# Two groups of filler matmuls divided otherwise near the end of a fused attention and soft-MoE kernel

## The chip, the cores and the metric

The kernel runs on one core of one Trainium2 chip. The core has a matrix engine (TensorE, in the profile PE for its matmuls and PEld for its weight loads), VectorE (DVE), ScalarE (ACT), GpSimd (POOL) and SyncE (SP, which here only issues DMAs), and 16 DMA engines. The metric is the device time of one execution in microseconds (us). Before the change the median of 4 runs is 302.89 us, with 301.69 us the lowest and 304.32 us the highest.

## What is computed

The reference is attention with a soft cap on the scores, whose output is the input of a mixture of experts with soft slots:

```
scores = cap * tanh(q @ k^T / sqrt(64) / cap)          # 8 batches x 12 heads, 448 x 448, cap = 30
attn   = softmax(scores) @ v                           # head size 64
x      = attn, heads side by side                      # 3584 tokens x 768
logits = x @ phi                                       # 3584 x 32 slots, 8 experts with 4 slots each
d = softmax over the tokens;  c = softmax over the slots
slot_input = d^T @ x                                   # 32 x 768
slot_out[e] = relu(slot_input[e] @ w1[e]) @ w2[e]      # hidden size 1024
out    = c @ slot_out                                  # 3584 x 768, float32
```

## The kernel before

The attention covers 48 pairs of heads. Each pair has 7 tiles of 64 keys from each head of 448 keys, which makes 336 tiles, taken in an order that interleaves the two pairs of a quad. Six tiles are a chunk, so there are 56 chunks (NCH = 56, numbered 0 to 55). For a chunk TensorE makes scores in two halves of three tiles (`qk_chunk`, L316), ScalarE applies tanh (`tanh_chunk`, L325) and, for most tiles, exp (`exp_part`, L329). In some chunks one or two tiles get their exp as a polynomial on VectorE instead (`poly_exp`, L359 to L364). Two chunks later TensorE multiplies the result with v (`pv_mms`, L382), VectorE divides by the row sums (`norm`, L389 and L392), and GpSimd casts the next v (`vcast`, L286).

Everything that is not in this main loop hangs on named slots. `at(j, slot, f, ...)` puts a call into chunk j's slot, and `run(j, slot)` issues it when the loop comes by. The order of work on every engine is thus written out by hand: an engine takes its instructions in this order, and nothing rearranges them later. The slot "d" of a chunk comes after the second `qk_chunk` of that chunk, so at the very end of it; the next thing on TensorE that needs its own place is `pv_first` in the chunk after.

Among the calls are filler matmuls, whose results nobody reads. `fill` adds them into unused columns of the bank of the product with v. `spare(n, parts)` takes a tile of 128 x (128 * parts) from the pool `psV`, with the tag "pv", and calls `busy(n, tile)`. That pool has one buffer, so a `spare` tile has to wait until VectorE has read the product with v before it, and the next product with v has to wait until the filler is written. In `busy` a tile wider than 128 columns is served with n // 3 matmuls of 384 columns (L626) and n % 3 of 128 columns (L629). A tile of 128 columns is served with n matmuls of 128 columns (L629). Each matmul has a weight load of its own ahead of it.

After the last chunk come the last two pairs' products with v (tiles `pvm` and `pvl`), the last logits and slot sums (`slpl`), the experts' first layer (`layer1`, tile `hp`, L820, in four groups of 24 matmuls: two halves for experts 0 to 3, two for experts 4 to 7), its relu (L831 on ScalarE, L834 on VectorE), the second layer (`layer2`, `so_ps`, L853) and the output (L885 to L945). The second layer's weights were partly put aside in DRAM and come back as `w2t` by DMAs that SP issues (L799). The output is 3584 x 768 float32, stored from L869 and L886.

Of the kernel before, what the change touches and what calls it, by code (L numbers as in the profile page):

```python
# [36 lines left out]
def kernel(  # L37
# [27 lines left out]
    NCH = NTILE // CH  # L65
# [473 lines left out]
    def at(j, slot, f, *a):  # L539
        if j < 0:  # L540
            j, slot = 0, "b"
        aux.setdefault((j, slot), []).append((f, a))
# [21 lines left out]
    for b in range(B):  # L564
        j, p = b * PER, 6 * b
# [36 lines left out]
        at(1 + n * (NCH - 5) // len(wjobs), "b", *job)  # L602
    for j, slot, n in ((0, "a", 10), (0, "c", 10), (1, "b", 10), (1, "c", 8)):
        at(j, slot, spare, n, 1)
    for j, slot, n, parts in ((NCH - 6, "d", 8, 3), (NCH - 4, "d", 8, 3), (NCH - 2, "d", 12, 1)):
        at(j, slot, spare, n, parts)
    at(0, "c", init_vbd, 0)
    at(1, "c", init_vbd, 1)
# [376 lines left out]
```

## Time and profile before

| | |
|---|---|
| median of 4 runs | 302.89 us (301.69 to 304.32) |
| the profiled execution | 302.53 us |
| its span, from first to last instruction | 300.7 us |
| TensorE matmuls busy | 266.2 us, 4828 matmuls, 4828 weight loads |
| ScalarE busy | 265.0 us |
| VectorE busy | 231.2 us |
| GpSimd busy | 137.6 us |
| DMA | 68.52 MB, mean 228 GB/s |
| 384-column fillers L626 on `junk` | 67 matmuls, 14.2 us busy |
| 128-column fillers L629 on `junk` | 77 matmuls, 8.1 us busy |

The span lies 1.8 us below the profiled execution's time; what is outside it is start and end of the program. Busy time is the union of an engine's instructions, so that matmuls which overlap in the array count once. The profile gives each matmul the time from its start until its result is complete, which is longer than the distance at which the next one can follow. A line of a timeline has start, duration, engine, source line, operation, output and inputs, and how many instructions it merges; in brackets stands the idle time before it and what ended it. In the chain of work that ended last, "issue" is time in which an engine waited for nothing that the profile shows.

### The profile page before, as it was taken

To read this page: it belongs to the slowest core of one execution; us is meant where nothing else is said; L and a number is where in the kernel's file an instruction comes from. 1 tells how busy PE (TensorE), PEld (TensorE's weight loads), DVE (VectorE), ACT (ScalarE), POOL (GpSimd) and SP (SyncE) were. 2 spreads that over 40 slices of the span, in tenths; PEclk is the share of its full clock that TensorE was granted. 3 is DMA by queue.
4 is the path that set the end of the run, shared out by engine and by line. 5 is a ranking of instruction groups with operands and counts; after the bars stand their busy time and mean duration, and the time that the engine had idled before them with its cause. 6 is when DMAs were issued, how large, how long until landed. Compare 5 with 4: busy or idle time off the path is not lost.

```text
span 300.7 us, 10911 instructions
## 1 busy us (share of the span) xinstructions
PE 266.2 (89%) x4828; PEld 180.0 (60%) x4828; DVE 231.2 (77%) x397; ACT 265.0 (88%) x211; POOL 137.6 (46%) x200
## 2 busy tenths in 40 slices
PE   8898889998999999989999999899999999898720
PEld 5665566755775667566756665667666777442400
DVE  3717869799988998899989988998888854237830
ACT  4999999999999999999999999999999996137720
POOL 4583563864486457634764567365633310300000
PEclk9999999999999999999999999999999999999985
DMA  7999999999999999999999999999999479939995
GB/s 253 243 187 205 193 196 208 186 216 219 208 202 195 198 228 219 195 204 229 180 190 209 226 193 194 215 223 211 191 210 199 128 235 348 413 128 381 407 421 233
DMA packets 58703, 68.52 MB, mean 228 GB/s; under 512 B 4256, under 2 KB 54688, under 8 KB 58656
## 3 DMA queue, kind: packets, MB, share of 16 engines
q0 software_dynamic: 42448, 35.31, 76.6%
q1 hardware_dynamic: 15920, 32.28, 30.7%
q8 instruction: 38, 0.62, 0.8%
q10 hardware_dynamic: 288, 0.23, 0.2%
q14 instruction: 9, 0.07, 0.1%
HBM read 92.11 MB, written 19.66 MB: 372 GB/s over the span
## 4 chain that ended last, share of the span: by engine, by line
ACT 42%; PE 30%; DVE 15%; issue 4%; POOL 3%; DMA 2%; DVEq 0%; SPq 0%; ACTq 0%; POOLq 0%
ACT ex L325 22%; ACT ex L329 17%; PE pv L382 9%; PE sc L316 4%; DVE ex L364 2%; DVE xq L392 2%; DVE work L363 2%; PE so_ps L853 2%; PE hp L820 2%; POOL vbd L286 2%; PE xps L430 2%; PE pv L412 1%; DVE work L362 1%; PE kps L276 1%; ACT ob L945 1%
## 5 line engine op out<-in xcount | busy, mean ns | idle before, releaser
L325 ACT ACTIVATE ex<-sc 128x1344 bf16<-128x1344 f32 (+1 forms) x113 | 144.0, 1353 | 1.8 <-PE sc L316 1.8
L329 ACT ACTIVATE ex<-ex 128x2688 bf16<-128x2688 bf16 (+5 forms) x58 | 120.9, 2093 | 0.1
L382 PE MATMUL pv<-vbd,ex 128*128 128x130 bf16 (+1 forms) x1610 | 95.4, 211 | 8.5 <-POOL vbd L286 5.9
L382 PEld LDWEIGHTS <-ex 128*128 128x128 bf16 (+1 forms) x1680 | 76.1, 101 | 34.1 <-issue 9.1
L316 PE MATMUL sc<-qT,kT 64*64 64x448 bf16 x672 | 71.3, 359 | 1.6 <-ACT ex L325 0.6
L286 POOL CAST vbd<-vraw 64x896 bf16<-64x896 f32 x46 | 45.0, 978 | 52.5 <-PE pv L382 38.4
L364 DVE SCALAR_TENSOR_TENSOR ex<-work 128x896 bf16<-128x896 f32 (+1 forms) x31 | 31.3, 1009 | 0.2
L363 DVE SCALAR_TENSOR_TENSOR work<-work 128x896 f32<-128x896 f32 (+1 forms) x31 | 30.2, 974 | 0.1
L362 DVE SCALAR_TENSOR_TENSOR work<-work 128x896 f32<-128x896 uint16 (+1 forms) x31 | 30.2, 973 | 0.0
L392 DVE TENSOR_TENSOR xq<-pv,rec 128x448 bf16<-128x448 f32 x46 | 28.7, 624 | 1.5
L316 PEld LDWEIGHTS <-kT 64*64 64x64 bf16 x672 | 23.6, 105 | 6.4 <-issue 2.9
L116 POOL DMA_DIRECT2D w1b<-in_moe_w_dram x32 | 24.8, 776 | 0.0
L474 POOL COPY e<-E 128x512 bf16<-128x512 bf16 x9 | 6.6, 731 | 39.0 <-PE eps L493 21.0
L294 POOL MEMSET vbd<- 64x1 bf16 x22 | 2.1, 96 | 47.3 <-PE pv L382 47.3
L278 DVE COPY kT<-kps 128x896 bf16<-128x896 bf16 x23 | 14.2, 618 | 10.0 <-PE kps L276 9.9
L361 DVE TENSOR_SCALAR work<-work 128x896 uint16<-128x896 uint16 (+1 forms) x31 | 20.8, 670 | 0.4
L412 PE MATMUL pv<-ones 128*128 128x57 bf16 x496 | 20.6, 188 | 0.0
L443 DVE COPY xT<-xps 128x896 bf16<-128x896 bf16 (+1 forms) x24 | 14.3, 598 | 8.0 <-PE xps L435 8.0
L359 DVE TENSOR_SCALAR work<-ex 128x896 int32<-128x896 bf16 (+1 forms) x31 | 20.2, 652 | 0.1
L186 POOL DMA_DIRECT2D qb<-in_q_dram x22 | 16.6, 754 | 3.1 <-DVE kT L237 3.1
L412 PEld LDWEIGHTS <-ones 128*128 128x128 bf16 x496 | 17.4, 96 | 0.3
L120 POOL DMA_DIRECT2D w2d<-in_moe_w_dram x22 | 16.8, 786 | 0.0
(130 smaller groups left out, 329.7 us busy)
## 6 DMA issues: line engine op xcount, KB each, us to landing
w1b<-in_moe_w_dram POOLq DMA_DIRECT2D x32, 384.0 KB, 8.7
vraw<-in_v_dram SPq DMA_DIRECT2D x44, 224.0 KB, 6.0
w2d<-in_moe_w_dram POOLq DMA_DIRECT2D x22, 384.0 KB, 8.7
w2t<-w2d SPq DMA_DIRECT2D x22, 384.0 KB, 7.3
out_dram<-ob SPq DMA_DIRECT2D x7, 768.0 KB, 8.4
qb<-in_q_dram POOLq DMA_DIRECT2D x22, 224.0 KB, 7.6
kb<-in_k_dram POOLq DMA_DIRECT2D x22, 224.0 KB, 6.0
out_dram<-obh SPq DMA_DIRECT2D x23, 192.0 KB, 2.0
```

The lines of the kernel that those rows point to most:

```text
L116: pool.dma_start(out=w1b[e][:, js, fs], in_=w1r[:, e, js, fs])
L286: pool.tensor_copy(vbds[Q % 2][r, :, :, c0:c0 + DH], raw[r])
L316: pe.matmul(sc[cs, u, 0:S], qkT["k", Q][r, c, cs], qkT["q", Q][r, :, cs], start=True, stop=True)
L325: act.activation(exs[j][:, half * CS + u0:half * CS + u1, :], sc[:, u0:u1, 0:S], ACT.Tanh, scale=qk_scale / cap)
L329: act.activation(exs[j][:, u0:u1, :], exs[j][:, u0:u1, :], ACT.Exp, scale=cap)
L361: lambda: dve.tensor_scalar(b.bitcast(U16), w, 7, None, ALU.logical_shift_left),
L362: lambda: dve.scalar_tensor_tensor(p, f, p2, f, ALU.add, ALU.mult),
L363: lambda: dve.scalar_tensor_tensor(p, p, p1, f, ALU.add, ALU.mult),
L364: lambda: dve.scalar_tensor_tensor(t, p, p0, b, ALU.add, ALU.mult))
L382: pe.matmul(out_, exs[j][r, u, q0:q0 + (HP if tail else P)], v_, start=(c == 0 and g == gs[0] < NF), stop=(c == NT - 1), skip_group_check= ...
L392: dve.tensor_tensor(xq[Q][:, h, s0:s1, :], pv[:, 0:s1 - s0, 0:DH], rec.to_broadcast([P, s1 - s0, DH]), op=ALU.mult)
L412: pe.matmul(home, ones, ones[:, 0:512 - NT * W], start=False, stop=True, skip_group_check=True)
```

## The change

One line of the table that places three of the `spare` calls is changed:

```
-    for j, slot, n, parts in ((NCH - 6, "d", 8, 3), (NCH - 4, "d", 8, 3), (NCH - 2, "d", 12, 1)):
+    for j, slot, n, parts in ((NCH - 6, "d", 11, 3), (NCH - 4, "d", 8, 3), (NCH - 2, "d", 12, 3)):
         at(j, slot, spare, n, parts)
```

In chunk 50 the filler is 11 units of 128 columns where it was 8: three matmuls of 384 columns and two of 128, where there were two and two. In chunk 54 the filler keeps 12 units, but on a tile of 384 columns: four matmuls of 384 columns, where there were twelve of 128. Chunk 52's filler is the same. On TensorE the program has one matmul and one weight load more in chunk 50, and eight of each less in chunk 54: 9658 become 9644. The other engines have the same instructions in the same order.

## The prediction

> **What bounds the kernel now.** I read the page's slices first, for where each engine is full, then the chain that ended last around the two places, then TensorE's timeline there, and last the DMA queues.
>
> The page's rows of busy time in 40 slices of 7.5 us:
>
> ```profile
> PE   8898889998999999989999999899999999898720
> ACT  4999999999999999999999999999999996137720
> PEclk9999999999999999999999999999999999999985
> ```
>
> Chunk 50's filler runs at 227 us and chunk 54's at 245 us, in slices 31 and 33. ScalarE is full in both, and TensorE nearly so. ScalarE's last exp ends at 252.08 us, while TensorE still multiplies that chunk with v until 253.9, so from there on TensorE is the late one. The chain, in order of time, agrees:
>
> ```profile
> 241.00 0.79 PE pv L382 x12
> ...
> 243.43 0.77 PE pv L382 x11
> 244.55 0.64 DVE xq L392
> 245.23 0.86 PE junk L629 x12
> 246.13 0.84 PE pv L382 x12
> ...
> 257.45 2.72 PE hp L820 x48
> 260.16 1.04 issue
> 261.20 1.48 PE hp L820 x24
> ```
>
> Here the filler of chunk 54 is itself a link, between VectorE's division and the next product with v. Ten us later there is a hole of 1.04 us, "issue", between the second and third group of the experts' first layer. After it the chain goes on to the output, whose stores start at 268.7 us and keep the DMA engines full to 297 us, so what comes late at 261 us ends late.
>
> TensorE's timeline at the two fillers, and one from 217 us with four wide ones:
>
> ```profile
> 217.00 0.82 PE L626 MATMUL junk<-ones 128*128 128x384 bf16 x4
> ...
> 226.97 0.50 PE L626 MATMUL junk<-ones 128*128 128x384 bf16 x2
> 227.31 0.28 PE L629 MATMUL junk<-ones 128*128 128x128 bf16 x2
> 227.64 0.84 PE L382 MATMUL pv<-vbd,ex 128*128 128x130 bf16 x12
> ...
> 245.23 0.84 PE L629 MATMUL junk<-ones 128*128 128x128 bf16 x12 [0.40 <-DVE xq L392]
> 246.13 0.84 PE L382 MATMUL pv<-vbd,ex 128*128 128x130 bf16 x12
> ```
>
> **Chunk 54.** Twelve narrow fillers take 0.84 us, the last 0.22 of it the last one's own time, so they start (0.84 - 0.22) / 11 = 56 ns apart. By the first row wide ones start about (0.82 - 0.33) / 3 = 163 ns apart, the first distance of a group being 10 ns longer. The product with v waits until the last filler is written: 246.13 is 56 ns after 245.23 + 0.84. Four wide ones end at 245.23 + 0.17 + 2 x 0.163 + 0.326 = 246.05, and v follows at 246.11. The change is worth **-0.02 us**. That eight weight loads go too is worth nothing: narrow fillers run at one per 56 ns with a load each, so the loads are hidden behind the columns.
>
> **Chunk 50.** One wide filler more: **+0.163 us**. It stands ahead of the next product with v at 227.64. The cover would be ScalarE, which is fed two halves ahead and does not wait for TensorE between 215 and 252 us; but TensorE's later waits in this stretch (0.19 us at 231.64 for GpSimd's v, 0.40 at 245.23 for VectorE) are for work that TensorE's own products released, and move along. So I take it in full. The bounds are 0, if those loops had room, and 0.163.
>
> Up to 255 us the sum is +0.14 us.
>
> **The hole at 260.16.** The third group's first matmul waits by the program for TensorE's own earlier writes only, and those are complete at 260.11. What else can hold it is the program itself:
>
> ```profile
> q8 instruction: 38, 0.62, 0.8%
> ```
>
> This queue brings code: 38 packets of 16 KB. TensorE's 9684 instructions, its semaphore ones included, make 255 a packet, so I take this as TensorE's code in blocks of 256. I set the packets' starts in the trace against the number of TensorE instructions started by then. All 38 lie at or behind the counts 256 k - 64, by 0.26 to 4.13 us (median 2.7), as if each block were asked for when the one before is entered. One of these counts, 9152, is exactly the first matmul after the hole. Its block was due when count 8896 was passed, at 254.70 us; its packet started at 258.77 (4.07 us later), took 0.93, and the matmul went at 261.20, 1.50 us after that. In the other 36 such spans TensorE reached the next count 1.36 us or more after the packet's end, so nothing stood still. Here it runs 256 instructions in 5.4 us, while the DMA engines carry 412 GB/s, and the late packet shows.
>
> Without the hole the third group would start at about 260.17, so the hole costs 1.04 us.
>
> The change moves the instructions behind chunk 54 forward by 14 counts. The boundary then falls 14 instructions later in the work, before the eighth matmul of the third group, and the request is due at what was count 8910, the logits matmul at 255.00 rather than the z sums at 254.70. With the +0.14 that is 255.14, so 0.44 us later. With the same delay the block is there at 261.20 + 0.44 = 261.64. Seven matmuls are done by then; the eighth, which ran at 261.44 before, runs at 261.64. **Sum: +0.20 us**, in which the moved hole has nearly eaten the seven matmuls it no longer holds. The delay is the unknown. By the crossing after it (9152 at 261.20, packet at 264.71) it is 3.51 us, and the sum is 0.20 - 0.56 = -0.36. If the delay is under about 3.0 us the hole is gone: the eighth matmul at 260.17 + 0.14 + 0.24 = 260.55, 0.89 us earlier than before. I take 4.07, the row of this very block under the same load.
>
> [...] By the row one boundary of 38 costs 1.04 us, and I go by it.
>
> 302.53 + 0.20 = 302.73 for an execution like the profiled one; that execution is 0.36 below the median of the runs, so I forecast 302.89 + 0.20 = **303.1 us**.
>
> **The rivals.** *The hole closes.* For it: 25 of the 38 packets had a delay of under 3.0 us. Against: the two under this load had 4.07 and 3.51, and the request comes later than before. It gives -0.89, 302.0 us.
>
> *The hole isn't code.* It ends 0.26 us after VectorE's relu of the second group (260.19 + 0.75), which could release the third. Against it is the program, which has no such wait there. Then the hole keeps its place, and the change is the two fillers: +0.14, 303.0 us.
>
> *The hole grows and the clock falls.* TensorE's clock is 1.00 from 3.5 to 290.3 us, and halves 2.35 us after the last matmul ends at 287.9. If the block came 1.5 us later still than forecast, TensorE would stand idle from 260.6 to 263.1, 2.5 us, past that point. At the start half clock lasted from the first matmul at 0.78 to 3.54, 2.8 us; that long at half speed loses 1.4 us of the two layers. Sum 0.20 + 1.5 + 1.4 = +3.1, 306.0 us. The point from which it decides is an idle time of about 2.4 us. No packet had a delay as long as this needs (5.6 against 4.13).
>
> *The next block.* The block after it was there with 0.2 to 0.3 us to spare: packet end at 265.67, first use at 267.38, 1.70 later. Its request moves with the hole (+0.44), its use by 14 instructions (+0.3 to 0.4) and by +0.20, so it should hold; if the delay is 0.6 longer there is a second hole of about 0.5 us, 303.6.
>
> **How the numbers follow.** Hole moved, 303.1 with -0.36 to +0.6 around it: 0.58. Hole gone, 302.0: 0.18. Not code, 303.0: 0.10. A second hole, 303.6: 0.08. Clock, 306.0: 0.06. Around each there are some 0.4 us of the median's own uncertainty, since four runs spread from 301.69 to 304.32. The range 301.7 to 304.6 takes in all but the clock case and what is left at both ends. One per cent, 3 us, is about what a measurement of this kernel can tell from no change. Only the clock case passes it on the slow side, and on the fast side nothing I can name: faster 0.03, same 0.90, slower 0.07.
>
> **What would show it.** In the profile after: chunk 54's filler as L626 x4 ending 0.82 us after its start, v following 0.06 later; chunk 50's as L626 x3 with v 0.16 later against the filler's start; the hole between the seventh and eighth matmul of the third `hp` group (L820 split 55 and 41), and a code packet some 4 us after the logits matmul. A hole still between x48 and the third group shows that it wasn't code. I am wrong if the span differs by over 1.5 us, which would need idle time or half clock elsewhere than at 261 us.

## The result, and the profile after

The changed kernel takes 302.24 us in the median of 36 runs, the one before 301.98 us in the median of 55. The ratio is 1.0007 with a 95% interval of 0.9992 to 1.0022: no difference that can be told. The first four runs of before (302.89 us) had lain high. Of every kernel here but that with chunk 50 alone, 5 to 27% of the executions have a span above 301.7 us, and three of the profiles below (shifted by 24, without the `w2t` loads, and the second one of early 12 less) are such executions, in which everything stands 2.7 us or more later.

So the forecast of +0.20 us has +0.26 us beside it. The profile shows that this is a sum of other terms than the ones forecast. The profiled execution took 302.37 us (before: 302.53), but its span is 299.5 us where it was 300.7. The program is 1.2 us shorter from first to last instruction, and what lies outside the span grew from 1.8 to 2.9 us. Over all 36 executions the median span is 299.5 us and the median outside it 2.7; the kernel before has 300.1 to 300.2 and 1.86 in its later runs.

In the profiles TensorE has 9656 matmuls and weight loads before and 9642 after, both two lower than the numbers given with the change; the difference of 14 is the same.

The page's slices look as before:

```profile
PE   8898889998999999989999999899999999998820
ACT  4999999999999999999999999999999996237720
PEclk9999999999999999999999999999999999999995
```

The chain of the changed kernel, with start, duration, work and count:

```profile
227.03 0.59 PE junk L626 x3
227.79 0.85 PE pv L382 x12
...
244.68 0.64 DVE xq L392
245.37 0.84 PE junk L626 x4
246.25 0.84 PE pv L382 x12
...
257.56 3.09 PE hp L820 x55
260.69 1.24 PE hp L820 x17
```

The 1.04 us of "issue" between the second and third group of the first layer is gone. What is left of it stands between the 55th and the 56th matmul, that is between the seventh and the eighth of the third group, where the prediction put it. TensorE's timeline of the changed kernel has the two fillers:

```profile
226.96 0.66 PE L626 MATMUL junk<-ones 128*128 128x384 bf16 x3
227.46 0.28 PE L629 MATMUL junk<-ones 128*128 128x128 bf16 x2
227.79 0.85 PE L382 MATMUL pv<-vbd,ex 128*128 128x130 bf16 x12
...
245.37 0.82 PE L626 MATMUL junk<-ones 128*128 128x384 bf16 x4 [0.39 <-DVE xq L392]
246.25 0.84 PE L382 MATMUL pv<-vbd,ex 128*128 128x130 bf16 x12
```

From the filler's start to the product with v it is 0.83 us in chunk 50, where it was 0.67, and 0.88 in chunk 54, where it was 0.90: +0.16 and -0.02, as worked out. At the first layer the program is 0.12 us late (257.45 against 257.33; +0.14 forecast). That alone shows little, because the kernel before reaches it at 257.44 in its second profile. Counted from the start of chunk 50's filler the first layer begins 30.36 and 30.35 us later in the two profiles of before, and 30.49 in the changed kernel: +0.13.

**Where the rest of the time went.** From the first matmul of the first layer to the first of the second layer it took 6.88 us before and 6.00 after, of which 0.40 is hole (a layer without one takes 5.60 us). The first output matmul comes at 267.22 instead of 267.97. Then the stores begin, and something is given back there. These are SP's issues of an early store, before and after:

```profile
269.13 0.51 SPq L886 DMA_DIRECT2D out_dram<-obh  x1
```

```profile
268.37 1.08 SPq L886 DMA_DIRECT2D out_dram<-obh  x1
```

The second takes twice as long, while a code packet of 16 KB (267.71 to 269.10 in the trace) is under way. Before the change that packet (268.25 to 269.27) was over by the time the first store's data moved at 269.54. The point at which fewer than all 16 engines are busy comes at 297.21 before and at 296.85 after, so of the 0.75 us 0.4 is lost again. The end of the stores, by half microseconds, has in its last two columns the busy share of the 16 DMA engines and GB/s. Before:

```profile
297.00:297.50 0.50, 0.00 (x0) 0.00 (x0) 0.00 (x0) 0.00 (x0) 0.00 (x0) 0.50 0.54 213
297.50:298.00 0.50, 0.00 (x0) 0.00 (x0) 0.00 (x0) 0.00 (x0) 0.00 (x0) 0.50 0.09 31
298.00:298.50 0.50, 0.00 (x0) 0.00 (x0) 0.00 (x0) 0.00 (x0) 0.00 (x0) 0.50 0.06 25
298.50:299.00 0.50, 0.00 (x0) 0.00 (x0) 0.00 (x0) 0.00 (x0) 0.00 (x0) 0.50 0.08 31
```

After:

```profile
296.50:297.00 0.50, 0.00 (x0) 0.00 (x0) 0.00 (x0) 0.00 (x0) 0.00 (x0) 0.50 0.71 283
297.00:297.50 0.50, 0.00 (x0) 0.00 (x0) 0.00 (x0) 0.00 (x0) 0.00 (x0) 0.50 0.08 31
297.50:298.00 0.50, 0.00 (x0) 0.00 (x0) 0.00 (x0) 0.00 (x0) 0.00 (x0) 0.50 0.05 18
298.00:298.50 0.50, 0.00 (x0) 0.00 (x0) 0.00 (x0) 0.00 (x0) 0.00 (x0) 0.50 0.00 0
```

A share of 0.06 is one engine of 16. Before, one engine works alone from about 297.5 to 299.2; after, from 297.0 to 297.97. Before, a code packet that starts at 286.99 and takes 0.96 us lies under the stores, and the last engine is done about 2.0 us after the others; after, it is 1.1 us. In the changed kernel this packet starts at 301.33, 1.8 us after the last instruction, and the page counts one fewer inside the span:

```profile
q8 instruction: 37, 0.61, 0.8%
```

The last data of the stores land at 297.97 instead of 299.23. For the two profiled executions the terms are: start of the first layer +0.12, the layer -0.88, the stores until fewer than 16 engines are busy +0.40, the last engine -0.90, from the last data to the last instruction +0.1, outside the span +1.0. They add up to -0.16, from 302.53 to 302.37.

So there are four places where a code packet may cost time: (a) the hole in the first layer, (b) the first stores, (c) the last stores, (d) after the end.

### The profile page after: what moved, and what is told of

Read it like the earlier page. It is cut to its first block, busy times and chain, and to the rows that moved or that the text cites. A ratio compares the mean times of both kernels' runs of the same rounds, so it can differ in the third digit from the quotient of the medians.

```text
span 299.5 us, 10897 instructions
## 1 busy us (share of the span) xinstructions
PE 266.6 (89%) x4821; PEld 179.8 (60%) x4821; DVE 231.2 (77%) x397; ACT 265.0 (88%) x211; POOL 137.8 (46%) x200
## 4 chain that ended last, share of the span: by engine, by line
ACT 42%; PE 30%; DVE 15%; issue 4%; POOL 3%; DMA 2%; DVEq 0%; SPq 0%; ACTq 0%; POOLq 0%
ACT ex L325 22%; ACT ex L329 17%; PE pv L382 9%; PE sc L316 4%; DVE ex L364 2%; DVE xq L392 2%; DVE work L363 2%; PE so_ps L853 2%; PE hp L820 2%; POOL vbd L286 2%; PE xps L430 2%; PE pv L412 1%; DVE work L362 1%; PE kps L276 1%; ACT ob L945 1%
```

## The experiments

All of them change the number of TensorE's instructions, or what the code packets meet. A filler's columns stay the same in those that divide early fillers otherwise. Those fillers lie in chunks 0 to 27, at 8.8 to 127 us, where the loop is not late on TensorE: in the kernel before ScalarE is busy for 139.89 of the 140 us from 10 to 150. Each kernel was timed beside the kernel before on the same chip. The ratio compares these executions and is not the quotient of the two medians shown. In the table the span and the time outside it are medians over all timed executions of a kernel. "First layer" is the time from its first matmul to the second layer's first in the profiled execution; it is 5.60 us where there is no hole.

| kernel | TensorE instructions against before | median us (before beside it) | ratio, 95% interval | span | outside | first layer |
|---|---|---|---|---|---|---|
| before, once more | 0 | 302.06 (302.00) | 1.0009, 0.9983 to 1.0034 | 300.2 | 1.85 | 5.98 |
| shifted by 24 | +24 | 301.83 (302.00) | 0.9988, 0.9967 to 1.0009 | 300.0 | 1.86 | 5.59 |
| shifted by 144 | +144 | 302.29 (302.00) | 1.0021, 0.9999 to 1.0043 | 300.45 | 1.86 | 5.60 |
| chunk 50 alone | +2 | 302.26 (302.00) | 1.0003, 0.9984 to 1.0022 | 300.45 | 1.88 | 6.36 |
| chunk 54 alone | -16 | 301.50 (302.06) | 0.9988, 0.9967 to 1.0008 | 299.5 | 1.88 | 5.61 |
| before, early 12 less | -12 | 301.31 (302.06) | 0.9975, 0.9958 to 0.9992 | 299.3 | 2.00 | 5.78 |
| the change and early 44 less | -58 | 302.17 (302.06) | 1.0005, 0.9987 to 1.0024 | 300.3 | 1.88 | 5.75 |
| without the `w2t` loads | 0 | 301.39 (302.06) | 0.9970, 0.9949 to 0.9991 | 299.6 | 1.78 | 5.60 |
| the change, once more | -14 | 302.30 (302.08) | 1.0003, 0.9975 to 1.0032 | 299.8 | 2.59 | 5.64 |
| early 12 less, once more | -12 | 301.40 (302.08) | 0.9971, 0.9950 to 0.9993 | 299.2 | 2.03 | 6.11 |
| before, early 8 less | -8 | 302.10 (302.08) | 0.9991, 0.9969 to 1.0013 | 300.25 | 1.85 | 6.03 |
| before, early 20 less | -20 | 301.28 (302.08) | 0.9970, 0.9948 to 0.9992 | 299.3 | 1.86 | 5.60 |

**The kernel before, once more.** No edit.

> The kernel before, once more, for the spread of its own executions. All theories: ratio 1.000 within 0.002. The code theory: in its profile the hole stands again between the second and third group of the first layer (L820 split 48 and 48) if the code packet comes more than about 3.0 us after the boundary at 254.7 us, and is smaller or absent if it comes sooner; the hole's size is (packet's delay - 3.0) us. The theory that the hole is a wait for the relu: 1.0 us in every execution.

In its profiled execution the packet for the block at count 9152 came 3.32 us after its boundary, where it had been 4.07. TensorE's timeline:

```profile
257.44 2.77 PE L820 MATMUL hp<-w1b,slT 128*32 128x512 bf16 x48
260.41 1.48 PE L820 MATMUL hp<-w1b,slT 128*32 128x512 bf16 x24 [0.20 <-PE hp L820]
```

The break is at the same place, but the third group comes 2.97 us after the first matmul, where it had come 3.87. Without a hole the third group comes 2.60 us after (runs with 144 more and with 20 less), so the hole is 0.37 us here and was 1.27 in the first profile. The same program has holes of different sizes, which a fixed wait would not give. VectorE's relu of the second group runs here from 260.30 to 261.05 us and ends after the third group has started at 260.41, so it is not what releases it. The profile that the prediction rested on had the longest hole of all that were taken.

**All boundaries moved by 24 and by 144 instructions.** Early fillers divided into narrow matmuls:

```
+                narrow = f is spare and slot == "a" and b in (1, 2)
-                at(j + k, slot, f, n)
+                at(j + k, slot, f, *((n, 1) if narrow else (n,)))
```

```
-            at(j + 1, "d", spare, 34)
+            at(j + 1, "d", spare, 34, 1)
...
+                narrow = f is spare and (b < 3 or (b == 3 and slot == "c"))
-                at(j + k, slot, f, n)
+                at(j + k, slot, f, *((n, 1) if narrow else (n,)))
```

> The kernel before, with two fillers of chunks 13 and 20 (10 units each) divided into 10 matmuls of 128 columns where they were three of 384 and one of 128: the same columns, 24 TensorE instructions more, far ahead of the place where TensorE is late. The code theory: every block boundary falls 24 instructions earlier in the work; the one at 260 us then lies 12 matmuls before the end of the second group of the first layer, its block is asked for at 254.4 us and due at 259.3, 4.9 us apart where it was 5.5, so the hole is 0.5 us larger (1.6 at a delay of 4.07) and splits L820 into 36 and 60; time +0.3 to +0.6 us, ratio 1.001 to 1.002. The theory that the hole is a wait for the relu or of a fixed place: hole unmoved at 48 and 48, 1.0 us, ratio 1.000. The theory that the end is set by something else than this chain: the hole moves, ratio 1.000.

> The kernel before, with all wide fillers of chunk 1, the groups of 10 and 14 units in chunks 6, 13 and 20 and that of 14 in chunk 27 divided into matmuls of 128 columns: the same columns, 144 TensorE instructions more, all before 150 us. The code theory: the boundaries that were at counts 8896 and 9152 lie at 8752 and 9008 in the old count, 6.1 us apart, and the next span is 6.1 us as well, where the worst one had 5.5; the hole at L820 is gone and at a delay of 4.07 one of 0.4 us stands ahead of L820, so 0.6 to 1.0 us less, ratio 0.997 to 0.998. The fixed-place theory: hole unmoved, ratio 1.000. The theory that the end is set by something else: no hole at L820, but ratio 1.000 within 0.001.

With 144 the hole in the first layer is gone, as the code theory has it, three groups in one piece (the edit adds a line, so L820 is L821 here):

```profile
257.44 4.07 PE L821 MATMUL hp<-w1b,slT 128*32 128x512 bf16 x72
```

But the kernel is not faster. It comes to the output at 266.81 us, 0.37 earlier than the run before it, and yet its span is longer. One of SP's issues in the first stores of this kernel (L869 in the others):

```profile
270.38 2.19 SPq L870 DMA_DIRECT2D out_dram<-obh  x1
```

An issue of these stores takes 0.41 us in the kernel before (median of 25). Here a code packet starts at 270.51 and takes 1.70 us, and SP's issue takes 2.19. The DMA engines run dry meanwhile, in windows of 1 us:

```profile
270.00:271.00 1.00, 1.00 (x19) 0.43 (x17) 0.62 (x1) 0.58 (x1) 0.00 (x0) 1.00 1.14 399
271.00:272.00 1.00, 1.00 (x14) 0.34 (x18) 0.00 (x0) 0.59 (x2) 0.00 (x0) 1.00 0.33 123
272.00:273.00 1.00, 0.82 (x10) 0.12 (x3) 0.55 (x2) 0.87 (x2) 0.00 (x0) 1.00 0.05 11
```

Against the second profile of before, place (b) loses 1.43 us (from the first matmul on L889 to the point at which fewer than 16 engines are busy); place (a) gains 0.38, and the last stores, under which no packet lies, 1.01. The theory as it was put, with place (a) alone, is refuted by the time: 0.6 to 1.0 us less was expected. With 24 the hole that should have grown to 1.6 us was not there at all in the profiled execution, which is one of the late ones, and the time was 301.83 us, not 0.3 to 0.6 more. The packet's delay was 1.66 us, not 4.07. My assumption of a fixed delay at this load is what fails here.

**The two parts of the change alone.**

```
-    for j, slot, n, parts in ((NCH - 6, "d", 8, 3), (NCH - 4, "d", 8, 3), (NCH - 2, "d", 12, 1)):
+    for j, slot, n, parts in ((NCH - 6, "d", 11, 3), (NCH - 4, "d", 8, 3), (NCH - 2, "d", 12, 1)):
```

> Only chunk 50's filler is changed, 11 units for 8. My sum: the product with v after it 0.16 us later against the filler's start, all that follows 0.16 later, boundaries 2 instructions earlier in the work (one matmul), hole unchanged within 0.05 us at the same delay; +0.16 to 0.2 us, ratio 1.0005. If the waits of the loop absorb the filler: 0, ratio 1.000.

The ratio of 1.0003 has room for both answers (0.9984 to 1.0022), but the trace has not: from the start of chunk 50's filler to the first layer it is 30.51 us, where the two profiles of before have 30.36 and 30.35. The loop did not absorb the filler. The hole stands before the 48th matmul of the first layer, one earlier than before, as two instructions more should have it.

```
-    for j, slot, n, parts in ((NCH - 6, "d", 8, 3), (NCH - 4, "d", 8, 3), (NCH - 2, "d", 12, 1)):
+    for j, slot, n, parts in ((NCH - 6, "d", 8, 3), (NCH - 4, "d", 8, 3), (NCH - 2, "d", 12, 3)):
```

> Only chunk 54's filler is changed: 16 TensorE instructions less than before, the program's end 2 instructions nearer to the block boundary than in the changed kernel. Theory A (what the changed kernel does to the time is where the program's end lies to a block boundary): 2.5 to 2.9 us outside the span instead of 1.86, span 299.3 to 299.7 in the executions without a late start, time within 0.4 us of before. Theory B (the filler of chunk 54 or that of chunk 50 by its own work shortens the span): the time outside the span 1.86; the span 0.02 us shorter apart from the hole. My recorded sum without chunk 50: hole moved by eight matmuls, +0.04 us in the span.

The span shrinks to 299.5 us as theory A has it, but the time outside stays at 1.88, which theory A did not expect. Its program ends two instructions earlier than the changed kernel's. In the trace its last packet starts at 291.54 us, still under the stores, and one or two engines work on for 1.9 us after the others at the end. The shorter first layer (5.61) pays for that in the profiled execution. The ratio alone tells nothing (0.9967 to 1.0008).

**The change of the count, without the two fillers.** One filler of chunk 1 divided otherwise, both late fillers as before:

```
-    for j, slot, n in ((0, "a", 10), (0, "c", 10), (1, "b", 10), (1, "c", 8)):
-        at(j, slot, spare, n, 1)
+    for j, slot, n, parts in ((0, "a", 10, 1), (0, "c", 10, 1), (1, "b", 10, 3), (1, "c", 8, 1)):
+        at(j, slot, spare, n, parts)
```

> The kernel before with both late fillers as they were; one filler of chunk 1 (10 units) is divided into three matmuls of 384 columns and one of 128 instead of ten of 128: 12 TensorE instructions less, at 10 to 20 us, where TensorE is not late. Theory A: as the changed kernel, 2.5 to 2.9 us outside the span and a span of 299.3 to 299.7, although no filler of the changed ones is touched; a last code packet after the end of the span. Theory B: as before, span 300.05 and 1.86 outside, ratio 1.000.

Without a touch to the two fillers this kernel shows what the changed one shows: a span shorter by 0.9 us, a last packet after the end (300.83, the span ends at 299.05), and a time outside that reaches 3.22 us. Its median of 2.00 is less than the 2.5 to 2.9 that theory A had. Theory B falls. This one is faster than before by 0.25%, clear of noise, and so it is in its second measurement (below).

**The changed kernel with 44 instructions less in the beginning**, so that it ends before a boundary:

```
     for j, slot, n in ((0, "a", 10), (0, "c", 10), (1, "b", 10), (1, "c", 8)):
-        at(j, slot, spare, n, 1)
+        at(j, slot, spare, n, 3)
```

> The changed kernel with the four fillers of chunks 0 and 1 divided into wide matmuls as well: 44 instructions less again, so that the program ends before the block boundary. Theory A: no code packet behind the last matmul nor after the end, 1.86 us outside the span again, span 299.3 to 299.7; time 301.2 to 301.5, ratio 0.998, faster than both kernels. Theory B: outside 1.86, and whatever the span does it is by the hole alone; with the boundary 58 instructions further in the work than before and 5.44 us between request and need it is as large as before.

Theory A fails here, with 302.17 us where 301.2 to 301.5 was expected. There is no packet after the last matmul nor after the end, 1.88 us outside, and yet a span of 300.3. It is place (b) again: its packet starts at 268.67, and SP's issue of the third store takes 1.65 us.

```profile
268.83 1.65 SPq L869 DMA_DIRECT2D out_dram<-obh  x1
```

In the same microseconds before, once more, has the first row, this kernel the second:

```profile
270.00:271.00 1.00, 1.00 (x18) 0.45 (x18) 0.75 (x2) 0.71 (x2) 0.00 (x0) 1.00 1.05 393
```

```profile
270.00:271.00 1.00, 1.00 (x18) 0.45 (x18) 0.75 (x2) 0.71 (x2) 0.00 (x0) 1.00 0.08 18
```

TensorE, VectorE and ScalarE are as busy in both; only the DMA engines stand. From this and the run with 144 comes theory C, that all four places count.

**No loads under the packets.** The kernel leaves out the 22 loads of `w2t`; its second layer multiplies with the ten kept parts over again, so part of its result is other numbers.

```
-    for n0, half in sorted(w2_spilled, key=lambda x: (x[1], x[0])):
+    for n0, half in ():
```

> The kernel before without the 22 loads of the second layer's put-aside weights (the second layer multiplies with the ten kept parts over again, so that part of the result is other numbers). The code theory: with no loads on the DMA queues at 250 to 266 us the packet of the block at 9152 starts within 1.5 us of its boundary at 254.7, no hole at L820, and the next packet as soon. If the delay of the packet has nothing to do with the loads: delay 3 to 4 us and a hole of up to 1 us as before.

A window of this kernel where the loads were:

```profile
255.00:260.00 5.00, 5.00 (x100) 3.71 (x96) 1.48 (x6) 1.66 (x5) 0.12 (x1) 1.00 0.01 3
```

The packet starts 0.92 us after its boundary (258.02 in this execution), and the hole is gone. So I take most of the delay of 2.9 to 4.1 us in most of the other kernels for time behind these transfers. That is inferred from this one profile, and the kernel shifted by 24 had 1.66 us with the loads in place. The kernel gains 0.7 us in all, more than the hole of 0.37 us in the second profile of before; what else gains was not taken apart.

**Four instructions to either side.** The next four were timed together on one chip.

> The changed kernel once more, on the chip of the next three. Theory C (the time moves with four code packets: the one of the hole in the first layer, the one at the first stores, where SP's issue is held, the one under the last stores, which leaves one DMA engine late, and one after the end): span 299.3 to 299.6 without a late start, 2.3 to 2.9 us outside it, time 302.0 to 302.3. If the excess outside the span in the first measurement was that chip's: 1.86 outside and 301.4.

> The kernel before with one filler of chunk 1 divided otherwise, 12 instructions less, once more. Theory C: last code packet at or after the program's end and none under the last stores, 301.1 to 301.5, ratio 0.997 to 0.998. If the first result was chance: ratio 1.000.

The changed kernel has again 2.59 us outside, with a span 0.4 shorter than the 300.2 beside it. The run with 12 less is again faster, 0.9971.

```
-    for j, slot, n in ((0, "a", 10), (0, "c", 10), (1, "b", 10), (1, "c", 8)):
-        at(j, slot, spare, n, 1)
+    for j, slot, n, parts in ((0, "a", 10, 1), (0, "c", 10, 1), (1, "b", 10, 1), (1, "c", 8, 3)):
+        at(j, slot, spare, n, parts)
```

> The kernel before with the filler of 8 units in chunk 1 as two matmuls of 384 columns and two of 128 instead of eight of 128: 8 instructions less, 4 more than in the run before it. Theory C: the last boundary is crossed with the last matmuls instead of after them, its packet runs under the last stores (287 to 290 us), one DMA engine is late by 0.7 to 1.0 us, span 300.0 to 300.2, 1.86 outside, time 301.9 to 302.1, ratio 1.000: 0.6 us over the run with 12 less. If fewer instructions, or the wide fillers of chunk 1 themselves, are the gain: 301.5 to 301.7, between the two.

With 8 less, four instructions from the run with 12 less, the gain is gone: 302.10 against 301.40, as theory C said. Its last packet starts at 288.21, and one or two engines are late again:

```profile
297.00:297.50 0.50, 0.00 (x0) 0.00 (x0) 0.00 (x0) 0.00 (x0) 0.00 (x0) 0.50 0.14 53
297.50:298.00 0.50, 0.00 (x0) 0.00 (x0) 0.00 (x0) 0.00 (x0) 0.00 (x0) 0.50 0.10 31
298.00:298.50 0.50, 0.00 (x0) 0.00 (x0) 0.00 (x0) 0.00 (x0) 0.00 (x0) 0.50 0.06 25
```

```
-    for j, slot, n in ((0, "a", 10), (0, "c", 10), (1, "b", 10), (1, "c", 8)):
-        at(j, slot, spare, n, 1)
+    for j, slot, n, parts in ((0, "a", 10, 1), (0, "c", 10, 1), (1, "b", 10, 3), (1, "c", 8, 3)):
+        at(j, slot, spare, n, parts)
```

> The kernel before with both of these fillers of chunk 1 divided so: 20 instructions less. Theory C: the boundary before the stores is crossed 8 instructions further in the work than in the run with 12 less, at the first output matmuls, its packet starts at 268.4 us or later, and one of the first store issues on SP takes 1.0 to 1.7 us where 0.4 is usual, with the DMA engines idle meanwhile; no packet under the last stores; span 299.6 to 300.2, time 301.6 to 302.2, ratio 0.999 to 1.000. If fewer instructions are the gain: below the run with 12 less, 301.0.

Half of this was wrong. There is no packet under the last stores and none after the end; but the packet at the first stores starts at 267.38, not at 268.4 or later, and SP's longest issue is 0.97 us, just short of what I had expected to be the least; and the time is 301.28, where 301.6 to 302.2 was expected. The end of its stores:

```profile
296.00:296.50 0.50, 0.00 (x0) 0.00 (x0) 0.00 (x0) 0.00 (x0) 0.00 (x0) 0.50 1.02 412
296.50:297.00 0.50, 0.00 (x0) 0.00 (x0) 0.00 (x0) 0.00 (x0) 0.00 (x0) 0.50 0.06 19
297.00:297.50 0.50, 0.00 (x0) 0.00 (x0) 0.00 (x0) 0.00 (x0) 0.00 (x0) 0.50 0.08 31
297.50:298.00 0.50, 0.00 (x0) 0.00 (x0) 0.00 (x0) 0.00 (x0) 0.00 (x0) 0.50 0.00 0
```

The kernel is 0.30% under before beside it (0.08 to 0.52%). It has the lowest median of the kernels that compute everything, though not to be told from that with 12 less. Both this and the run with 12 less beat the two kernels of the case, by dividing fillers at the other end of the program. That it gains as much as 12 less and not more speaks against the number of instructions as such.

**The four places in all 14 traces.** The packets and issues of the 14 profiles, set side by side, put the four places to the test.

- (a) Where a hole of over 0.1 us is left, the matmul of the first layer before which it stands follows the count, one matmul for two instructions: 47 matmuls ahead of it with 2 more, 48 in the kernel before (twice), 52 with 8 less, 54 with 12 less (twice), 55 with 14 less. With 58 less it lies between the third and the fourth group.
- (b) In 12 traces SP is issuing an early store when the packet ends, and in all 12 that issue ends 0.36 to 0.37 us later. It takes 0.40 to 2.19 us. Whether the packet holds the issue, or both wait for a third thing, is not shown. From the first matmul on L889 to the point at which fewer than 16 engines are busy it takes 28.73 to 28.76 us in the kernel before (twice) and in the two traces where the packet is over before the first issue. In the others it is longer by what the issue takes beyond about 0.67 us: by 0.42 in the changed kernel, 0.99 with 44 less, 1.44 with 144 more.
- (c) From that point to the last data it takes 1.71 to 2.02 us in the seven traces with a packet under the last stores, and 0.95 to 1.17 in the seven without.
- (d) In the four traces with a packet after the last instruction (the changed kernel and 12 less, each twice) the packet ends 3.09, 3.18, 3.09 and 2.33 us after the span, and the time outside is 2.85, 2.94, 2.85 and 2.09: 0.24 less each time. In the ten others it is 1.78 to 1.87.

## Why the prediction was right, and where not

The range held, no difference was forecast, and +0.20 us was the number. Only part of it was right for its reasons, and that the sum came within 0.06 us of the measured difference is luck: terms of up to 1 us that it did not have cancel in it.

- **The two fillers.** +0.163 and -0.02 were worked out, +0.16 and -0.02 stand in the timeline, and counted from chunk 50's filler the first layer begins 0.13 us later where +0.14 was forecast. That ScalarE and the loops behind VectorE and GpSimd would not absorb the filler was right: with chunk 50 alone it is +0.15.
- **The hole is code.** Right. It moved to between the seventh and eighth matmul of the third group, to the very instruction, and does so in the other kernels too; it changes from execution to execution with the packet's delay (1.27 us of hole at 4.07, 0.37 at 3.32 in the kernel before); and it is gone in the profile without the loads (delay 0.92). The rival of a fixed place falls.
- **The hole's size.** Wrong. "I take 4.07, the row of this very block under the same load" is the step that failed. The delays of this block were 3.32 in the kernel before, once more, 3.07 and 2.88 in the changed one, and 3.41 with chunk 50 alone and with 8 less. 4.07 was the longest seen. The eighth matmul ran at 260.69, not 261.64. The rival in which the hole closes (-0.89) came close: -0.75.
- **The hole's price.** I reckoned 1.04 us, since the third group's first matmul has a wait for TensorE's own writes. Without a hole the groups follow in one piece (2.60 us from the first matmul to the third group), so that wait costs nothing, and the hole was 1.27.
- **What comes late ends late.** Too simple. From 268 us the stores decide, and code packets fall together with delays there in two places that the prediction did not look at: an issue of SP at the first stores (1.08 us in the changed kernel, 0.51 before), and the last data, which come 2.02 us after all 16 engines were last busy before and 1.12 after. I had the list of packets, with 268.25 and 286.99 in it, and asked only what TensorE waits for.
- **The sum against the execution.** "302.53 + 0.20" took the 1.8 us outside the span as fixed. It is 1.75 to 1.92 us in every execution of the kernels that do not end near a block boundary, but 1.88 to 3.58 in the changed kernel. Beside each other on one chip the medians of the changed kernel are 0.4 us lower for the span and 0.7 us higher outside it; that of the time is 0.22 higher. This term, which was not in the sum, gave the forecast's sign.
- **The clock.** The deciding point of about 2.4 us of idle time was an estimate from one row. From the last matmul's end to the end of full clock it is 2.35 us before, but 3.69 in the changed kernel (287.15 to 290.84), so a fixed point there is not shown. TensorE stands idle for over 1.5 us nowhere between its matmuls in these two profiles.

Weighed against the runs, most of the 38 blocks cost nothing that the traces show. In the first profile and in that of the changed kernel TensorE stands waiting at the crossing of one count alone, 9152, with a packet that ended 1.50 and 1.62 us before; the other costs are at the places above. The two fillers alone were +0.14 us, and the measured +0.26 (ratio 0.9992 to 1.0022) can't tell it from +0.20; the holes in the traces can.

Open is why a packet comes so late. With 14 and with 12 less the last count (9664, as the prediction counts them) is passed at 286.7 and 286.2 us in their first profiles, some 6 and 8 instructions before the program's end, and the packet starts more than 14 us later, behind the last instruction. With 16 less it comes at 291.54 and with 8 less at 288.21, both under the stores. Nor is it known why the time outside is 2.6 us in the median with 14 less and 2.0 with 12 less. That it follows this packet's end is shown by the four traces, but the packet was not taken away alone. Which of the 16 DMA engines a code packet is on was not to be seen, so that it is the late one under the last stores is inferred.

## What to carry to other kernels

In this long unrolled program the position of an instruction counted from the start was itself a parameter: there is a 16 KB packet for about every 255 TensorE instructions (38 for 9684), and where the packets fell, a hole of up to 1.27 us on TensorE, an issue of SP of up to 2.19 us, or last data up to 2.02 us after all 16 DMA engines were last busy went with them. When a change that should cost nothing moves the time by tenths of a per cent, set the packets of the instruction queues against the stretches where DMA or TensorE is the limit, and try moving the boundaries by dividing fillers far away before believing in the change. And of a sum that comes out right, compare the terms: span and time outside it went in opposite directions here.

## What the runs showed of the hardware

- An issue of a store on SP that was under way when a code packet ended went on for 0.36 to 0.37 us after it, in 12 traces of 12 at the first stores. It took 1.65 us with 44 less and 2.19 with 144 more instead of 0.4, and the DMA engines fell to a share of 0.08 and 0.05 over a microsecond.
- In the first profile every packet started 0.26 to 4.13 us behind the count at which the block ahead of it was entered, which fits a block asked for one block ahead, though the traces show the packet alone and not the request; without the `w2t` loads (DMA share 0.01) it was 0.92 us at the first layer. At the program's end that does not hold: in the changed kernel the last packet came 14.7 us behind its count. From a packet's end to the first use of its block passed 1.26 us or more in all 14 traces, also where TensorE stood waiting for it.
- The trace's record of TensorE's full clock begins at 3.54 us in the first profile, where the 128-column matmuls of the start go from 107 ns apart to 56 ns. It begins at 13.2 to 13.4 us in three profiles (shifted by 24, without the `w2t` loads, early 12 less once more) and at 3.5 to 5.0 in the eleven others. With the shift by 24 TensorE has 27 matmuls from 4 to 8 us and 30 from 8 to 12, where the first profile has 36 and 54. In the three the 21st tanh started at 44.7 to 44.8 us instead of 41.9 to 42.2. The kernel before has executions of that length too, so no edit brings them.
